# Channel attention with a squared-ReLU network: one sum and four softmax steps placed behind two PSUM additions, a bank copy ahead of a rounding step, a maximum ahead of four sums

## The chip, the core and the metric

One core of one Trainium2 chip runs the kernel. The metric is device time in microseconds (us), the median of three runs. TensorE (PE in the profile) multiplies, VectorE (DVE) and ScalarE (ACT) work on tiles, GpSimd (POOL) and SyncE (SP) issue the DMAs.

## What is computed

```
B, N, C = 4, 6080, 256;  d_ff = 2048;  everything float32
qn = q / (norm(q, axis=1) + 1e-6);  kn = k / (norm(k, axis=1) + 1e-6)
s  = kn^T @ qn / tau                       # 256 x 256 for each batch
a  = softmax over the last axis of s (max taken out, 1e-9 added to the sum)
x  = v @ a                                 # 6080 x 256 for each batch
out = max(x @ w_in, 0)^2 @ w_out           # w_in 256 x 2048, w_out 2048 x 256
```

## The kernel before

The attention matrix a and w_in of a batch are multiplied first (W = a w_in), so that the network runs on v itself: h = v W, out = max(h, 0)^2 w_out. A product in float32 is made of three products of rounded parts: each operand is split into a high part (a rounding cast, mostly on ACT) and a low part (the difference, on DVE).

v is cut into 48 blocks of 512 tokens (480 in the last two blocks of a batch), and the 2048 hidden channels into four groups of 512. The first two blocks and the last are done by plain products. The 45 blocks between make 180 **periods**, one for each block and group of channels. A period computes its piece of h with seven products in place of eight (a Strassen scheme), six matmuls of 128 x 256 for each, in three PSUM banks that the trace calls ps_b, ps_h and ps_c. The order in `period` (lines 1250 to 1334) is:

1. the first product into ps_b; ACT copies the bank to ps_c (the **bank copy**, "COPY ps_c<-ps_b") because later products add to both;
2. a product into ps_h, copied by ACT to the tile x; then a window of products with w_out for an earlier period (`window_S`, ps_o);
3. a product on top of ps_c, one on top of ps_b, one on top of ps_h; DVE adds ps_h to x (the **H addition**, "x<-x,ps_h");
4. a product on top of ps_c; DVE adds ps_c to x (the **C addition**, "x<-x,ps_c");
5. the products with w_out for the last period's rounded squares A (`window_A`), a last product on top of ps_c, which may begin only when the C addition has read the bank, and another window of products with w_out (`window_S` with the sums S).

Relu and square turn x into the squares. Beside their own rounding (`hi_A`, `lo_A`), sums of squares are needed for the windows S: `first_sums`, `third_sum` and `last_sum`, all on DVE ("x<-x" with nothing else), and the sums are split by `hi_S` (ACT, "s_hi") and `lo_S` (DVE, "s_lo<-x,s_hi"). `last_sum` finishes S1 and S2 of the period before (k-1). Where `plain(k - 1)` holds (the groups 0 and 1 of batches 0 to 2, and all groups in the first block) the sums are half as wide (256 elements for a partition instead of 512).

All engines keep the order in which the code records instructions. No scheduler moves them, so a line that is written earlier runs earlier on its engine, and an instruction that waits holds all that is behind it on that engine.

The softmax and W of the next batch (`softmax_and_W`) run beside the periods. The function is a generator: `yield from step(b, i, point)` hands control back until the period reaches a named point, and `side(point)` in `period` goes on with it there. The points come in the order "dve" (behind the first sums), "sq" (behind the C addition), "pe", "act" (before `window_A`), "mid" (behind the high part of A). Its steps: the maximum nx of the squared norms with a small number (reads the bank that the next period calls ps_b), three Newton steps for the inverse root of the norms, the inverse norms as a diagonal matrix (`diag`), the scaled scores, the negative row maximum (`negmax`), the exponentials, the reciprocal of their sum, and the transposed exponentials, cast to eT_hi and eT_lo (DVE) for the products with w_in (ps_w). In the trace the softmax of batch 1 stands at about 411 to 480 us, of batch 2 at 918 to 985 us, of batch 3 at 1422 to 1490 us.

The order written out in `period` that the change touches is this (from lines 1260 to 1315, shortened):

```
scalar.copy(C, B2)                     # bank copy
if prev and after_copy(k - 1): hi_A(k - 1, late_A)
...
third_sum(k - 1)
if plain(k - 1): last_sum(k - 1)
...
vector.tensor_add(s, s, H)             # H addition
if prev and not plain(k - 1): last_sum(k - 1)
product(k, C, S3, T3)
vector.tensor_add(s, s, C)             # C addition
side("sq")
lo_S(k - 1, "S1"); hi_S(k - 1, "S2")
square(k, a0)
```

In the trace nearly all instructions carry the line 27 of the recording layer; the tiles tell them apart. `hi_A` of a period is either called at its end or, where `after_copy` holds, in the next period behind the bank copy.

Of the kernel before, what the change touches and what calls it, by code (L numbers as in the profile page):

```python
# [8 lines left out]
F32 = mybir.dt.float32  # L9
# [21 lines left out]
def kernel(  # L31
# [22 lines left out]
    tensor, vector, scalar, pool_engine = (  # L54
        InProgramOrder(tc, e) for e in (nc.tensor, nc.vector, nc.scalar, nc.gpsimd)
    )
# [4 lines left out]
    NC = C // P  # L61
# [34 lines left out]
    small_tile = lambda name, b, cols, dt=F32: smalls.tile([P, cols], dt, tag=name, name=f"{name}{b}", bufs=1)  # L96
# [11 lines left out]
    def bank(name):  # L108

        at = banks["turn"] = (banks["turn"] + 1) % 3  # L110
        return ps_h.tile([P, T], F32, tag=f"h{at}", name=name)
# [72 lines left out]
    def switch_w_out(k):  # L184

        if k < GPB or k >= len(groups) or plain(k) == plain(k - GPB) or groups[k][2] in EARLY:
            return
        j = groups[k][2]
        if plain(k):
            reload_w_out(j)  # L190
            return
        for kept, part in zip(ws_kept[j], (wo_hi, wo_lo)):
            sync.dma_start(A21_of(part, j).bitcast(F32), kept)
# [123 lines left out]
    def reload_w_in(b, g):  # L317
        parts = wi_next[b, g] = wi_tiles(b, g)
        for kept, part in zip(wi_kept[g], parts):
            nc.sync.dma_start(part.bitcast(F32), kept)  # L320
# [208 lines left out]
    def until(point):  # L529

        while now["at"] != point:
            yield
# [53 lines left out]
    def step(b, first, point):  # L586

        if b == 0:
            for i in range(first):
                yield i > 0  # L590
        else:
            yield
            yield from until(point)

    def softmax_and_W(b):
# [4 lines left out]
        ps_n = ps_h.tile([P, T], F32, tag="h0", name=f"ps_n{b}") if b else bank(f"ps_n{b}")  # L600
        for m in range(2 * NC):
            tensor.matmul(
                ps_n[:, m : m + 1],
                acc[:, 1 - m // NC, 0, (m % NC) * P : (m % NC + 1) * P],
                ones[:, 0:1],
                start=m == 0,
                stop=True,
                skip_group_check=True,
            )
        yield from step(b, 2, "mid")  # L610
        if b:
            reload_w_in(b, 0)
        small = lambda name, dt=F32: small_tile(name, b, 2 * NC, dt)
        x = small("nx")

        vector.tensor_scalar_max(x, ps_n[:, 0 : 2 * NC], 2.0**-100)

        seed_i, y = small("nseed", I32), small("ny")
        vector.tensor_scalar(
# [7 lines left out]
            yield True  # L627
        for it in range(3):
            if it and b:
                yield from step(b, 1, "mid" if it == 1 else "dve")  # L630
            vector.tensor_mul(s_, x, y)
            vector.scalar_tensor_tensor(u_, s_, -0.5, y, op0=ALU.mult, op1=ALU.mult)
            vector.scalar_tensor_tensor(y, u_, 1.5, y, op0=ALU.add, op1=ALU.mult)
            if it == 1 and b == 0:
                yield False
# [16 lines left out]
        tensor.matmul(ps_b[:, 0:C], ones, diag.rearrange("p h c -> p (h c)"), start=True, stop=True)  # L652
        yield from step(b, 2, "mid")
        vector.tensor_mul(s, s, ps_b[:, 0:C].unsqueeze(1).broadcast_to([P, NC, C]))
        yield from step(b, 0, "dve")
        negmax = small_tile("negmax", b, NC)
        vector.tensor_reduce(negmax, s, axis=AX.X, op=ALU.max, negate=True)
        yield from step(b, 1, "act")
# [2 lines left out]
        for h in range(NC):  # L661
            scalar.activation(
                e[:, h, :], s[:, h, :], AF.Exp, bias=negmax[:, h : h + 1], accum_out=rsum[:, h : h + 1]
            )
        yield from step(b, 2, "dve")
        rinv = between.tile([P, NC], F32, tag="rinv", name=f"rinv{b}", bufs=1)
        vector.tensor_scalar_add(rsum, rsum, 1e-9)
        vector.reciprocal(rinv, rsum)
# [2 lines left out]
        for h in range(NC):  # L671
            for d in range(NC):
                tensor.transpose(
                    ps_t[:, d * C + h * P : d * C + (h + 1) * P], e[:, h, d * P : (d + 1) * P], ident
                )
        yield from step(b, 2, "dve")
        eT_hi = pool.tile([P, NC, C], F32R, tag="eT_hi", name=f"eT_hi{b}", bufs=1)
        eT_lo = pool.tile([P, NC, C], F32R, tag="s", name=f"eT_lo{b}", bufs=1)
        ps_tv = ps_t.rearrange("p (d c) -> p d c", d=NC)
# [278 lines left out]
    ORD = 1  # L958
    AT = (0, 0, 24, 26)
    AFTER_FROM = (12, 12, 12, 0)  # L960
    FREE_FROM = (12, 12, 12, 0)
    FREE = lambda k: groups[k][0] < B - 1 and groups[k][2] == 3 or groups[k][1] >= FREE_FROM[groups[k][0]]
    BS = (B - 1,)
# [5 lines left out]
    groups = [(b, n, j) for b, n in order[OLD:-1] for j in range(GPB)]  # L969
# [27 lines left out]
    def two_halves(tag, name):  # L997

        return ps_h.tile([P, 2, T // 2], F32, tag=tag, name=name)
# [5 lines left out]
    def half_of(k):  # L1005
        return blocks[groups[k][1]][1] // 2
# [34 lines left out]
    def plain(k):  # L1041

        b, n, j = groups[k]
        return (b, n) == order[OLD] if j in EARLY else n < FROM[j][b]
# [109 lines left out]
    a1, a0, a2, a3 = range(4)  # L1154

    def evict_C21(k):
        scalar.activation(XG[k][:, :, a2, :], C2.pop(k)[:, :, : half_of(k)], AF.Relu)
# [6 lines left out]
    def square(k, at):  # L1164
        s = XG[k][:, :, at, :]
        scalar.activation(s, s, AF.Square)

    def sum_of(k, to, one, other, op):

        x = XG[k][:, 0 : 1 if plain(k) else 2]  # L1170
        op(x[:, :, to, :], x[:, :, one, :], x[:, :, other, :])
# [8 lines left out]
    def third_sum(k):  # L1180
        sum_of(k, a2, a2, a1, vector.tensor_add)

    def last_sum(k):
        sum_of(k, a3, a3, a2, vector.tensor_sub)
# [10 lines left out]
    def hi_A(k, which):  # L1195
        s, at = which
        n = 1 if plain(k) else 2
        scalar.copy(PA[k, "A"][0][:, 0:n, at, :], XG[k][:, 0:n, s, :])
# [17 lines left out]
    def side(point):  # L1216

        now["at"] = point
        next(beside, None)
        if forming and next(forming[0], "end") == "end":  # L1220
            forming.pop(0)
# [23 lines left out]

    def after_copy(k):

        return not plain(k) and k < len(groups) - 1 and groups[k][1] >= AFTER_FROM[groups[k][0]]

    def period(k, before=nothing, w1=None, wa=None, w3=None):  # L1250

        now["k"] = k
        switch_w_out(k + 1)
        b, n, j = groups[k]
        half = half_of(k)
        prev = k > 0
        B2 = two_halves("h0", f"ps_b{k}")
        product(k, B2, A11, B11, start=True)
        C2[k] = C = two_halves("h2", f"ps_c{k}")
        scalar.copy(C[:, :, :half], B2[:, :, :half])  # L1260
        if prev and after_copy(k - 1):
            hi_A(k - 1, late_A)
        H = two_halves("h1", f"ps_h{k}")
        product(k, H, S1, T1, start=True)
        load_forms(k + 1, 1)
        x = XG[k] = pool.tile([P, 4, 2, half], F32, tag="x", name=f"x{k}").rearrange("p s r t -> p r s t")
        scalar.copy(x[:, :, a3, :], H[:, :, :half])
        if w1 is None and not plain(k - 2):
            copy_output(k - 2, 0)
        if prev:  # L1270
            if ORD and after_copy(k - 1):
                first_sums(k - 1)
                lo_A(k - 1, late_A)
            else:
                lo_A(k - 1, late_A)
                first_sums(k - 1)
        side("dve")
        late_step(last=True)
        if prev:
            third_sum(k - 1)  # L1280
            if plain(k - 1):
                last_sum(k - 1)
        v_step(k, "dve")
        (w1 or (lambda: window_S(k - 2, "S2")))()
        before()
        product(k, C, S2, T2)
        scalar.copy(x[:, :, a1, :], C[:, :, :half])
        if w1 is None:
            copy_output(k - 2, 0)
        load_forms(k + 2, 0)  # L1290
        late_step()
        if k >= len(groups) - 2:
            reload_w_out(k - len(groups) + 2)
        product(k, B2, A12, B21)
        if prev:
            hi_S(k - 1, "S1")
        scalar.activation(x[:, :, a0, :], B2[:, :, :half], AF.Relu)
        if w1 is None:
            copy_output(k - 2, 1)
        product(k, H, S4, B22)  # L1300
        s = x[:, :, a1, :]
        vector.tensor_add(s, s, H[:, :, :half])
        if FREE(k):
            scalar.activation(s, s, AF.Relu)
            square(k, a1)
        if prev and not plain(k - 1):
            last_sum(k - 1)
        product(k, C, S3, T3)
        s = x[:, :, a3, :]
        vector.tensor_add(s, s, C[:, :, :half])  # L1310
        side("sq")
        if prev:
            lo_S(k - 1, "S1")
            hi_S(k - 1, "S2")
        square(k, a0)
        relu_squares(k)
        if prev:
            lo_S(k - 1, "S2")
        side("pe")
        side("act")  # L1320
        v_step(k, "act")
        (wa or (lambda: window_A(k - 1)))()
        parts_tile(k, "A")
        hi_A(k, early_A)
        side("mid")
        v_step(k, "mid")
        lo_A(k, early_A)
        late_step()
        product(k, C, A22, T4)
        evict_C21(k)  # L1330
        square(k, a2)
        if not after_copy(k):
            hi_A(k, late_A)
        (w3 or (lambda: window_S(k - 1, "S1")))()
# [56 lines left out]
    for i in range(PAIR):  # L1391
        part = i % 2
        b, n, f = steps[i]
# [57 lines left out]
    for g in range(len(groups)):  # L1451
        b, n, j = groups[g]
# [16 lines left out]
    b, n = order[-1]  # L1469
# [77 lines left out]
```

## Time and profile before

| | |
|---|---|
| time, median of 3 runs | 2139.51 us (2138.34, 2139.51, 2139.69) |
| span of the profiled execution | 2137.0 us |
| time of the profiled execution itself | not listed apart; the median of the runs lies 2.5 us over its span |
| TensorE (PE) busy | 2123.9 us, 99%, 16990 matmuls |
| VectorE (DVE) busy | 1947.1 us, 91% |
| ScalarE (ACT) busy | 1818.6 us, 85% |
| GpSimd (POOL) busy | 403.4 us, 19% |
| chain that ended last | PE 89%, DVE 6%, ACT 2%, DMA 2%, issue 1% |

PE is busy in nearly the whole span. A row's duration overlaps the next row of its engine: matmuls of 256 columns are shown with .28 us and start every .12 us; DVE operations of 512 elements are shown with .68 us and start every .60 us. Times between rows are therefore taken from start to start.

### The profile page before, as it was taken

What the parts mean: (1) busy time and instruction counts of PE and PEld (TensorE: products, weight loads), DVE (VectorE), ACT (ScalarE), POOL (GpSimd) and SP (SyncE); (2) the same over time, 40 slices, a digit from 0 to 9 for tenths busy, and PEclk for the clock granted to TensorE, in tenths of its full rate; (3) what the DMA queues carried; (4) which work ended last, traced back from release to release, by engine and by line L of the source; (5) the groups of instructions that cost most, each with busy time, mean ns of one, the idle gap of its engine ahead of it and who ended that gap; (6) DMA issues with size and microseconds to landing.
All of it is one profiled execution on the core that took longest, in us unless ns stands there. A gap on an engine that the chain in (4) does not pass through costs nothing.

```text
span 2137.0 us, 43905 instructions
## 1 busy us (share of the span) xinstructions
PE 2123.9 (99%) x16990; PEld 2066.1 (97%) x16990; DVE 1947.1 (91%) x2577; ACT 1818.6 (85%) x2708; POOL 403.4 (19%) x506
## 2 busy tenths in 40 slices
PE   9999999999999999999999999999999999999999
PEld 8789999999999999999999999999999999999998
DVE  6898999998999999988999999999899999999993
ACT  5887888888888888878888888878888999999995
POOL 0000121211222121221222121121212122122121
PEclk9999999999999999999999999999999999999999
DMA  9777888889998888788999788887999788788783
GB/s 345 234 232 264 240 255 252 235 239 283 303 297 262 251 251 262 234 241 247 292 303 288 248 255 257 249 234 229 325 322 314 233 241 252 220 247 248 233 256 86
DMA packets 258865, 548.24 MB, mean 257 GB/s; under 512 B 26848, under 2 KB 120672, under 8 KB 258656
## 3 DMA queue, kind: packets, MB, share of 16 engines
q1 hardware_dynamic: 193696, 449.32, 62.3%
q0 software_dynamic: 64960, 96.11, 20.9%
q8 instruction: 134, 2.20, 0.4%
q14 instruction: 75, 0.61, 0.1%
HBM read 431.75 MB, written 64.23 MB: 232 GB/s over the span
## 4 chain that ended last, share of the span: by engine, by line
PE 89%; DVE 6%; ACT 2%; DMA 2%; issue 1%; SPq 0%; DVEq 0%; ACTq 0%
PE ps_o L27 41%; PE ps_c L27 16%; PE ps_h L27 14%; PE ps_b L27 11%; PE gram L27 4%; DVE x L27 2%; PE ps_w L27 2%; PE ps_o_m L27 1%; ACT x L27 1%; DMA wf<-wf_kept 1%; DVE s_lo L27 1%; DVE acc L27 1%; DMA qk<-in_k 1%; DVE A_lo L27 0%; DMA qk<-in_q 0%
## 5 line engine op out<-in xcount | busy, mean ns | idle before, releaser
L27 DVE TENSOR_TENSOR s_lo<-x,s_hi 128x1024 fp32r<-128x1024 f32 (+1 forms) x384 | 464.0, 1208 | 44.4 <-ACT s_hi L27 44.1
L27 PE MATMUL ps_c<-v_hi,wf 128*128 128x256 f32 (+1 forms) x2160 | 466.9, 280 | 4.4 <-DVE x L27 2.2
L27 POOL DMA_DIRECT2D o<-o x225 | 245.4, 1253 | 1102.7 <-ACT o L27 689.7
L27 ACT CAST s_hi<-x 128x1024 fp32r<-128x1024 f32 (+1 forms) x384 | 399.7, 1041 | 37.6 <-DVE x L27 27.9
L27 DVE TENSOR_TENSOR x<-x 128x1024 f32<-128x1024 f32 (+3 forms) x540 | 389.6, 722 | 10.3
L27 PEld LDWEIGHTS ps_c<-v_hi,wf 128*128 128x128 f32 x2160 | 367.4, 188 | 7.8 <-ACT ps_c L27 3.3
L27 ACT ACTIVATE x<-x 128x512 f32<-128x512 f32 (+2 forms) x540 | 350.0, 648 | 21.7 <-DVE x L27 9.2
L27 PE MATMUL ps_b<-v_hi,wf 128*128 128x256 f32 (+1 forms) x1440 | 309.7, 279 | 1.8 <-DVE nx L27 1.1
L27 PE MATMUL ps_h<-v_hi,wf 128*128 128x256 f32 (+1 forms) x1440 | 309.1, 278 | 0.0
L27 PE MATMUL ps_c<-v_lo,wf 128*128 128x256 f32 (+1 forms) x1080 | 300.9, 279 | 0.0
L27 DVE TENSOR_TENSOR A_lo<-x,A_hi 128x1024 fp32r<-128x1024 f32 (+3 forms) x360 | 276.9, 792 | 18.8 <-ACT A_hi L27 15.3
L27 ACT CAST A_hi<-x 128x1024 fp32r<-128x1024 f32 (+3 forms) x360 | 254.4, 707 | 38.4 <-DVE x L27 25.5
L27 PEld LDWEIGHTS ps_b<-v_hi,wf 128*128 128x128 f32 x1440 | 245.2, 188 | 2.3 <-DVE nx L27 1.3
L27 PEld LDWEIGHTS ps_h<-v_hi,wf 128*128 128x128 f32 x1440 | 244.9, 188 | 0.0
L27 ACT COPY x<-ps_c 128x512 f32<-128x512 f32 (+1 forms) x180 | 105.1, 584 | 158.3 <-PE ps_c L27 158.0
L27 PEld LDWEIGHTS ps_c<-v_lo,wf 128*128 128x128 f32 x1080 | 203.2, 188 | 0.1
L27 PE MATMUL ps_b<-v_lo,wf 128*128 128x256 f32 (+1 forms) x720 | 200.6, 279 | 0.0
L27 PE MATMUL ps_h<-v_lo,wf 128*128 128x256 f32 (+1 forms) x720 | 200.4, 278 | 0.0
L27 DVE TENSOR_TENSOR x<-x,ps_h 128x512 f32<-128x512 f32 (+1 forms) x180 | 122.4, 680 | 76.9 <-PE ps_h L27 76.6
L27 PE MATMUL ps_o<-s_hi,wo_hi 128*128 128x256 f32 (+3 forms) x954 | 190.1, 295 | 0.5 <-ACT s_hi L27 0.5
L27 PE MATMUL ps_o<-s_hi,wo_lo 128*128 128x256 f32 (+3 forms) x954 | 190.2, 295 | 0.0
L27 PE MATMUL ps_o<-s_lo,wo_hi 128*128 128x256 f32 (+3 forms) x954 | 190.0, 295 | 0.1
(166 smaller groups left out, 5166.9 us busy)
## 6 DMA issues: line engine op xcount, KB each, us to landing
wf<-wf_kept SPq DMA_DIRECT2D x360, 512.0 KB, 5.3
wf<-wf_kept SPq DMA_DIRECT2D x360, 384.0 KB, 4.9
o<-o POOLq DMA_DIRECT2D x114, 256.0 KB, 5.9
qk<-in_k SPq DMA_DIRECT2D x87, 256.0 KB, 4.3
qk<-in_q SPq DMA_DIRECT2D x87, 256.0 KB, 4.8
v<-in_vT POOLq DMA_DIRECT2D x76, 256.0 KB, 5.1
out_T<-o POOLq DMA_DIRECT2D x152, 128.0 KB, 4.7
o<-o POOLq DMA_DIRECT2D x76, 128.0 KB, 6.2
```

What stands on the lines that cost most here:

```text
L27: return lambda *args, **kwargs: self.tc.keep_in_program_order(issue(*args, **kwargs))
```

## The change

- `last_sum` of the period before is called behind both PSUM additions (H and C) for all periods, and the square of the part a0 (ACT) goes ahead of `hi_S(k - 1, "S2")`.
- Four of the softmax steps go from the point "dve" to the point "sq", which is now behind `last_sum`: the third Newton step with the diagonal, `negmax`, the reciprocal, and eT_hi with eT_lo.
- In the first nine periods `hi_A` of the period before stands behind the bank copy (`AFTER_FIRST`), and `first_sums` ahead of the late `lo_A`.
- nx is taken at the point "act" instead of "mid" for the batches 1 to 3.

```diff
+        small = lambda name, dt=F32: small_tile(name, b, 2 * NC, dt)
+        x = small("nx")
+        if b:
+            vector.tensor_scalar_max(x, ps_n[:, 0 : 2 * NC], 2.0**-100)
         yield from step(b, 2, "mid")
         if b:
             reload_w_in(b, 0)
-        small = lambda name, dt=F32: small_tile(name, b, 2 * NC, dt)
-        x = small("nx")
-
-        vector.tensor_scalar_max(x, ps_n[:, 0 : 2 * NC], 2.0**-100)
+        else:
+            vector.tensor_scalar_max(x, ps_n[:, 0 : 2 * NC], 2.0**-100)
...
-                yield from step(b, 1, "mid" if it == 1 else "dve")
+                yield from step(b, 1, "mid" if it == 1 else "sq")
...
-        yield from step(b, 0, "dve")
+        yield from step(b, 0, "sq")
         negmax = small_tile("negmax", b, NC)
...
-        yield from step(b, 2, "dve")
+        yield from step(b, 2, "sq")
         rinv = between.tile([P, NC], F32, tag="rinv", name=f"rinv{b}", bufs=1)
...
-        yield from step(b, 2, "dve")
+        yield from step(b, 2, "sq")
         eT_hi = pool.tile([P, NC, C], F32R, tag="eT_hi", name=f"eT_hi{b}", bufs=1)
...
+    AFTER_FIRST = 9
...
-        return not plain(k) and k < len(groups) - 1 and groups[k][1] >= AFTER_FROM[groups[k][0]]
+        return k < AFTER_FIRST or not plain(k) and k < len(groups) - 1 and groups[k][1] >= AFTER_FROM[groups[k][0]]
...
             third_sum(k - 1)
-            if plain(k - 1):
-                last_sum(k - 1)
         v_step(k, "dve")
...
-        if prev and not plain(k - 1):
-            last_sum(k - 1)
         product(k, C, S3, T3)
         s = x[:, :, a3, :]
         vector.tensor_add(s, s, C[:, :, :half])
+        square(k, a0)
+        if prev:
+            last_sum(k - 1)
         side("sq")
         if prev:
             lo_S(k - 1, "S1")
             hi_S(k - 1, "S2")
-        square(k, a0)
         relu_squares(k)
```

PE's order is the same in both programs, and so is POOL's. On VectorE at the step eT of batch 1 (period 28; x27 holds the squares and sums of period 27, x28 the tile of this period; ps_t1 the transposed exponentials) the order before is:

```order
L27 TENSOR_TENSOR x27_5402<-x27_5402 128x2x2x256
L27 CAST eT_hi1_5552<-ps_t1_5474 128x512
L27 TENSOR_TENSOR eT_lo1_5553<-ps_t1_5474,eT_hi1_5552 128x512
L27 TENSOR_TENSOR x27_5402<-x27_5402 128x512
L27 TENSOR_TENSOR x28_5548<-x28_5548,ps_h28_5537 128x512
L27 TENSOR_TENSOR x27_5402<-x27_5402 128x512
L27 TENSOR_TENSOR x28_5548<-x28_5548,ps_c28_5535 128x512
L27 TENSOR_TENSOR s1_lo_27_5587<-x27_5402,s1_hi_27_5586 128x1024
```

and with the change:

```order
L27 TENSOR_TENSOR x27_5402<-x27_5402 128x2x2x256
L27 TENSOR_TENSOR x27_5402<-x27_5402 128x512
L27 TENSOR_TENSOR x28_5548<-x28_5548,ps_h28_5537 128x512
L27 TENSOR_TENSOR x28_5548<-x28_5548,ps_c28_5535 128x512
L27 TENSOR_TENSOR x27_5402<-x27_5402 128x512
L27 CAST eT_hi1_5602<-ps_t1_5474 128x512
L27 TENSOR_TENSOR eT_lo1_5603<-ps_t1_5474,eT_hi1_5602 128x512
L27 TENSOR_TENSOR s1_lo_27_5583<-x27_5402,s1_hi_27_5582 128x1024
```

The two casts went from ahead of the third sum to behind the C addition and the last sum, while the products that read them (ps_w) keep their place on PE, directly behind the product that the C addition waits for. The same engine at the third Newton step of batch 1 (period 24), with the change (ns1 to nr1 and diag1 stood ahead of the second row, x23 128x512, before, and the fourth and third rows were in the other order):

```order
L27 TENSOR_TENSOR x23_4836<-x23_4836 128x512
L27 TENSOR_TENSOR x24_4971<-x24_4971,ps_h24_4960 128x512
L27 TENSOR_TENSOR x24_4971<-x24_4971,ps_c24_4958 128x512
L27 TENSOR_TENSOR x23_4836<-x23_4836 128x512
L27 TENSOR_TENSOR ns1_4777<-nx1_4754,ny1_4774 128x4
L27 SCALAR_TENSOR_TENSOR nu1_4778<-ns1_4777,ny1_4774 128x4
L27 SCALAR_TENSOR_TENSOR ny1_4774<-nu1_4778,ny1_4774 128x4
L27 TENSOR_TENSOR ns1_4777<-nx1_4754,ny1_4774 128x4
L27 TENSOR_SCALAR ns1_4777<-ns1_4777 128x4
L27 TENSOR_SCALAR ns1_4777<-ns1_4777,tau_sb_89 128x2
L27 RECIPROCAL nr1_5031<-ns1_4777 128x4
L27 TENSOR_SCALAR diag1_5033<-ident_82,nr1_5031 128x128 x2
```

Behind these rows stands s1_lo, the low part of S1. On ScalarE at the bank copy of period 8 (A_hi_7 is the rounding of period 7), before:

```order
L27 ACTIVATE x7_2437<-x7_2437 128x512
L27 CAST A_hi_7_2541<-x7_2437 128x2x256
L27 COPY ps_c8_2577<-ps_b8_2570 128x512
L27 COPY x8_2590<-ps_h8_2579 128x512
L27 COPY x8_2590<-ps_c8_2577 128x512
```

and with the change:

```order
L27 ACTIVATE x7_2437<-x7_2437 128x512
L27 COPY ps_c8_2576<-ps_b8_2569 128x512
L27 CAST A_hi_7_2541<-x7_2437 128x2x256
L27 COPY x8_2590<-ps_h8_2579 128x512
L27 COPY x8_2590<-ps_c8_2576 128x512
```

The copy and the rounding cast have changed places.

## Rows read from the trace of the kernel before

**Rows 1.** The profile page: its span, the busy time of each engine (with its share and number of instructions), and the granted TensorE clock in 40 slices, in tenths.

```profile
span 2137.0 us, 43905 instructions
PE 2123.9 (99%) x16990; PEld 2066.1 (97%) x16990; DVE 1947.1 (91%) x2577; ACT 1818.6 (85%) x2708; POOL 403.4 (19%) x506
PEclk9999999999999999999999999999999999999999
```

**Rows 2.** The waits of PE: what waited and for whom; us in total, times, longest.

```profile
PE ps_c L27 <- DVE x L27: 2.2, 5, 0.9
PE ps_c L27 <- ACT ps_c L27: 2.1, 3, 0.9
```

**Rows 3.** The timeline of VectorE in period 28, batch 1. Here and below the columns are start, duration, engine, line, operation, out<-in with its shape, count, and in brackets the idle time just before and what ended it.

```profile
476.01 0.69 DVE L27 CAST eT_hi<-ps_t 128x512 fp32r<-128x512 f32 x1
476.73 0.69 DVE L27 TENSOR_TENSOR eT_lo<-ps_t,eT_hi 128x512 fp32r<-128x512 f32 x1
...
477.94 0.68 DVE L27 TENSOR_TENSOR x<-x,ps_h 128x512 f32<-128x512 f32 x1
478.54 0.68 DVE L27 TENSOR_TENSOR x<-x 128x512 f32<-128x512 f32 x1
479.14 0.68 DVE L27 TENSOR_TENSOR x<-x,ps_c 128x512 f32<-128x512 f32 x1
```

**Rows 4.** The timeline of PE in the same period.

```profile
477.59 0.28 PE L27 MATMUL ps_c<-v_hi,wf 128*128 128x256 f32 x1
477.70 0.62 PE L27 MATMUL ps_w<-dec_w,eT_hi 128*128 128x512 f32 x2
478.16 0.61 PE L27 MATMUL ps_w<-dec_w,eT_lo 128*128 128x512 f32 x2
```

**Rows 5.** The timeline of PE and VectorE at the same step in batch 2.

```profile
983.68 0.28 PE L27 MATMUL ps_c<-v_hi,wf 128*128 128x256 f32 x1
...
984.00 0.69 DVE L27 TENSOR_TENSOR x<-x,ps_c 128x512 f32<-128x512 f32 x1
```

**Rows 6.** The timeline of VectorE around the third Newton step of batch 1, whose first row is ns at 432.70.

```profile
432.70 0.16 DVE L27 TENSOR_TENSOR ns<-nx,ny 128x4 f32<-128x4 f32 x1
...
434.56 0.69 DVE L27 TENSOR_TENSOR x<-x 128x512 f32<-128x512 f32 x1
...
436.96 1.22 DVE L27 TENSOR_TENSOR s_lo<-x,s_hi 128x1024 fp32r<-128x1024 f32 x1
438.10 1.22 DVE L27 SCALAR_TENSOR_TENSOR x<-x 128x1024 f32<-128x1024 f32 x1
```

**Rows 7.** The timeline of PE in the same period: the last product of the C addition, the last of window A, the product onto ps_c behind it, and the first that reads s_lo.

```profile
434.44 0.28 PE L27 MATMUL ps_c<-v_hi,wf 128*128 128x256 f32 x1
...
436.55 0.27 PE L27 MATMUL ps_o<-A_lo,wo_hi 128*128 128x256 f32 x1
437.10 0.39 PE L27 MATMUL ps_c<-v_hi,wf 128*128 128x256 f32 x1 [0.28 <-DVE x L27]
...
438.85 0.28 PE L27 MATMUL ps_o<-s_lo,wS_hi 128*128 128x256 f32 x1
```

**Rows 8.** The timeline of PE at the third Newton step of batch 2: the first product of window A and the first that reads s_lo.

```profile
942.81 0.39 PE L27 MATMUL ps_o<-A_hi,wo_hi 128*128 128x256 f32 x2
...
946.16 0.40 PE L27 MATMUL ps_o<-s_lo,wS_hi 128*128 128x256 f32 x2
```

**Rows 9.** The timeline of ScalarE at the bank copy of the period that follows the Newton step of batch 1.

```profile
441.23 0.41 ACT L27 CAST A_hi<-x 128x256 fp32r<-128x256 f32 x1
441.54 0.58 ACT L27 COPY ps_c<-ps_b 128x512 f32<-128x512 f32 x1
```

**Rows 10.** The timeline of PE there: the product onto ps_c that needs the copy.

```profile
442.17 0.39 PE L27 MATMUL ps_c<-v_hi,wf 128*128 128x256 f32 x1
```

**Rows 11.** The timeline of all engines where nx of batch 2 is taken.

```profile
924.92 1.80 DVE L27 TENSOR_TENSOR v<-v 128x256 f32<-128x256 f32 x4
...
925.46 0.28 PE L27 MATMUL ps_o<-s_lo,wo_hi 128*128 128x256 f32 x1
...
926.64 0.15 DVE L27 TENSOR_SCALAR nx<-ps_n 128x4 f32<-128x4 f32 x1
...
926.85 0.38 PE L27 MATMUL ps_b<-v_hi,wf 128*128 128x256 f32 x1 [1.11 <-DVE nx L27]
```

**Rows 12.** The timeline of all engines at a bank copy in the first nine periods.

```profile
250.85 0.62 ACT L27 CAST A_hi<-x 128x512 fp32r<-128x512 f32 x1
251.37 0.58 ACT L27 COPY ps_c<-ps_b 128x512 f32<-128x512 f32 x1
...
252.00 0.39 PE L27 MATMUL ps_c<-v_hi,wf 128*128 128x256 f32 x1 [0.92 <-ACT ps_c L27]
```

**Rows 13.** The timeline of VectorE and PE at a C addition whose last sum stood ahead of both additions.

```profile
615.00 0.89 DVE L27 TENSOR_TENSOR x<-x 128x256 f32<-128x256 f32 x2
...
616.40 0.68 DVE L27 TENSOR_TENSOR x<-x,ps_c 128x512 f32<-128x512 f32 x1
...
617.14 0.39 PE L27 MATMUL ps_c<-v_hi,wf 128*128 128x256 f32 x1 [0.42 <-DVE x L27]
```

**Rows 14.** The timeline of PE at a C addition in batch 3.

```profile
1689.00 0.28 PE L27 MATMUL ps_o<-A_lo,wo_hi 128*128 128x256 f32 x1
...
1689.19 0.39 PE L27 MATMUL ps_c<-v_hi,wf 128*128 128x256 f32 x1
```

## The prediction

> **What bounds the kernel now.** I read the page first. PE is busy in 2123.9 of 2137.0 us, 99% [rows 1], so time can be won or lost only where PE stands still. PE's order does not change; what the change can do is to move the moments at which VectorE and ScalarE release PE. The next view is therefore the waits of PE: the largest behind the start are products onto ps_c, 2.2 us in five waits for DVE's C addition and 2.1 us in three waits for ACT's bank copy [rows 2]. That is all that the moved sums and copies can win, apart from nx below and waits too short for that view. Then the timelines of the places that the edits touch, start to start, for PE and the engine that releases it. The rates I use from them: a matmul of 256 columns starts every .12 us and one of 512 columns every .23 [rows 4]; a VectorE step of 512 elements takes .60 (477.94 to 478.54) [rows 3], two sums of 256 together .80 [rows 13], a pass of 1024 takes 1.14 [rows 6]. The C addition starts .32 behind the start of the last product (983.68 to 984.00) [rows 5]. PE starts about .05 behind the end of what it waited for, and after a wait the next product comes about .11 later than the pace (437.10 carries .39 instead of .28) [rows 7].
>
> **The change part by part.** A positive number is time lost.
>
> *eT behind the last sum: +7.0.* Before, eT_hi starts at 476.01, over a microsecond ahead of the products that read it, at 477.70 [rows 3, 4]. Now it stands behind the C addition and the last sum, while ps_w stays directly behind the product that the C addition waits for. The last product starts at 477.59 [rows 4], the C addition at 477.91, the last sum at 478.51, eT_hi at 479.11; with its .69 [rows 3] and .05 PE goes on at 479.85 instead of 477.70: 2.15 of standing still. eT_lo comes .72 behind eT_hi [rows 3], while PE has only two products of .23 to do before it needs it: another .25 with the restart. Together 2.4. In batch 2 the last sum is half as wide: 984.00 + .60 + .40 + .69 + .05 = 985.74, against 983.80 [rows 5], 1.95 and .25, 2.2. Batch 3 has the same shape as batch 1, 2.4. Nothing covers this, since nothing that is ready stands on PE between the product and ps_w. Bounds 5.6 (no restart costs, C addition at once) to 7.6.
>
> By the rows a VectorE step of 512 elements holds its engine for .60 although its row says .68 to .69 [rows 3]; I use the starts. The Trainium skill, "VectorE: DVE Perf Modes", section "The DRAIN you can't avoid", says that the next operation does not start until the pipe is empty; by it, with the rows' full durations, the two steps ahead of eT_hi would each take .08 more, and this term would be about 7.5. The trace disagrees, since successive starts here are closer than one duration.
>
> *Third Newton step and diagonal behind the last sum: +1.7.* The block is 1.86 long (432.70 to 434.56) [rows 6]. It left room ahead of the H addition, which now begins earlier; but it goes ahead of s_lo. In batch 1: last product 434.44 [rows 7], C addition 434.76, last sum 435.36, block 435.96, s_lo 437.82 to 439.04, so PE can read it at 439.09. It needs it at 438.85 [rows 7], but .55 of that was a wait at 436.55 to 437.10 [rows 7], which is gone since the C addition is no longer behind the last sum: .43 and the restart. So need 438.30, wait .79 and restart .11, less .55: +.35. Batch 3 alike. In batch 2 the last product is at 942.69, one step ahead of window A [rows 8]; C addition 943.01, last sum 943.61, block 944.01, s_lo 945.87 to 947.09, PE at 947.14 against 946.16 [rows 8]: +1.0 with restart less a small wait saved. Sum 1.7, bounds .5 to 2.5.
>
> *What follows the late steps: +2.0.* The squares of the period (438.10) [rows 6] start at 438.95, .85 later; on ACT the rounding of A and the bank copy of the next period (441.54) [rows 9] follow. The product that needs the copy stood at 442.17 [rows 10] with a short wait; moved by .35 it would be at about 442.35, and the copy comes at 442.98 or so: about +.5. The same in batch 3, +.3 in batch 2 where PE has already waited more: together about 1.2. negmax is one pass over 512 elements, .60 by the row nearest to it [rows 3], in front of s_lo in the three batches; between nothing and all of it I take .27 each, .8. The reciprocal is of four numbers at most and is nothing beside it. Bounds 0 (ACT's slack takes it all) to 3.0.
>
> *nx ahead of v: -1.4.* In batch 2 nx, which frees the bank of ps_b, stood behind four sums of v (924.92 to 926.64), and PE stood from 925.46 to 926.85, 1.39 less a pace of .12 plus a restart of .1 [rows 11]. Now nx is issued ahead of them, about 1.7 earlier, and PE goes on without a wait. Batches 1 and 3 have no such row, 0. Bounds -1.4 and -1.0. The four sums move .2 back and are waited for by nothing near.
>
> *The C addition without the last sum ahead: -1.9.* At 616.40 the C addition stands behind two sums [rows 13]; one, .40, goes behind it, and PE at 617.14 waited .42 by its bracket: I take -.4 there and -.3 at a like place at 1629. In batch 3 nine places have a PE step from the last of window A to the next product onto ps_c of .19 or so instead of .12, and the next one a restart later [rows 14]: -.07 to -.18, together -1.2. Bounds -2.5 to -.7. In periods without such a wait the last sum goes from one place to another of the same engine, in front of s_lo. VectorE's idle time ahead of the H addition becomes longer and the time behind shorter by .60; s_lo is read some 1.9 us behind the product before window A (436.96 to 438.85) [rows 6, 7], so s_lo at the same time as before costs nothing.
>
> *Bank copy ahead of the rounding in nine periods: -1.1.* PE's three waits for this copy are 2.1 us [rows 2]; the brackets count from the modelled end, .16 behind the pace, and each has a restart, so 2.9 is the most there is. The copy goes ahead of one cast: .52 at 250.85 [rows 12], .31 where it is narrow [rows 9]. I take -.52 and twice -.31. The cast itself is then later by the copy's .52, and with it A_lo on VectorE, which is why I don't take more. Bounds -3.0 and 0.
>
> *Sum.* 7.0 + 1.7 + 2.0 - 1.4 - 1.9 - 1.1 = +6.3. Against the span of 2137.0, with the same 2.5 us outside it, that is 2143.3 and **2145.8** us as a time; the median of the runs, 2139.5, is that span with its 2.5.
>
> **The rivals.** A measurement of this kernel can tell some 0.2% from no change: 4.3 us, that is below 2135.2 or above 2143.8.
>
> *The copies and squares are in time.* The early squares on ACT and earlier copies make the follow-on 0, and the first nine periods give all of 2.9: 6.3 - 2.0 - 1.8 = +2.5, **2142.0**, not slower. For it: ACT is busy for 85% of the span [rows 1], and the first wait at each copy is a chain of ScalarE steps that gets shorter. Against: near 441 ACT's row order shows no room between cast and copy [rows 9].
>
> *eT is hidden.* If PE does not need eT directly behind the product, for example because ps_c's last product comes much later than in the rows, the 7.0 go: -.7, **2138.8**. Against: the order shows the same neighbours, and rows 4 and 5 have no gap.
>
> *The waits fall and eT is hidden.* The other side: the C addition decides more waits than the view names, since it stands in front of a product in all 180 periods; from the point at which eT_hi is ready by the time that PE has finished the product, the sum is 0 for the late steps and -1.4 - 1.9 - 2.9 = -6.2 or more, up to -8 with the last sum's .60 gained elsewhere: about **2132**, faster. For it: 2.2 us in five waits are named [rows 2]. Against: it needs VectorE over two microseconds ahead.
>
> *The clock falls.* The granted clock reads 9 in all slices, the upper level (2.4 GHz) [rows 1], though PE stood 1.39 us at a stretch [rows 11]. The new pauses are 2.15. If each brings PE to 1.2 GHz for about the length of a window A and the rest of its period, some 4 us, three times 4 us is +12: **2158**. The Trainium skill, "TensorE: Matmul & The Clock Gate", "Part 1: The HAM clock gate", says that the clock falls to its lower level after PE has idled; by it a pause could cost more than its length. No row of this trace shows it falling behind a pause.
>
> *The change does not do what it says.* Excluded by the order of the instructions, which shows each of the moves.
>
> **How the numbers follow.** The forecast, 2143.8 to 2148.5 by the bounds of its terms taken together: .52, and .04 for more of the same kind. Copies in time (2142.0, between 2139.5 and 2143.8): .22. eT hidden (2138.8): .09. The waits fall (2132): .10. The clock: .03. Slower is .52 + .04 + .03 = .59, same .22 + .09 = .31, faster .10. The range leaves out the fast case, the clock and the end of the forecast: 2138.0 to 2149.5.
>
> **What would show it.** Right: three waits "ps_w for DVE eT" of 1.9 to 2.2 us in the waits of PE, and VectorE's eT_hi behind the last sum; no wait for nx at 926; waits of s_lo of .8 to 1.1 behind the third Newton step; fewer waits of ps_c for DVE x. Wrong: no wait at ps_w, or a C addition that starts late in the other periods; PE's waits for ACT's copy as large as before would put the time at the upper end.

## The result

The changed kernel takes **2154.2 us** (median of 5 runs, 2151.7 to 2157.5); the kernel before took 2139.7 in its five. The ratio is 1.0070, with a 95% interval of 1.0057 to 1.0082: 14.5 us slower. The forecast was 2145.8, with a range to 2149.5: the direction was right, the size was not, and the time lies beyond the range.

The profiled execution has a span of 2153.7 us, 16.7 more than before; its own time is 2155.5, 1.3 above the median. These are its page's lines that answer to [rows 1], and after them the waits of PE (what waited, for whom; us in total, times, longest), which answer to [rows 2].

```profile
span 2153.7 us, 43914 instructions
PE 2131.0 (99%) x16990; PEld 2072.1 (96%) x16990; DVE 1942.8 (90%) x2577; ACT 1827.2 (85%) x2708; POOL 402.9 (19%) x506
PEclk9999999999999999999999999999999999999999
```

```profile
PE ps_w L27 <- DVE eT_lo L27: 7.9, 3, 2.7
PE ps_o L27 <- DVE s_lo L27: 2.2, 3, 0.9
PE gram L27 <- DMA qk<-in_q: 1.7, 2, 1.3
PE ps_c L27 <- ACT ps_c L27: 1.7, 4, 0.6
PE gram L27 <- DVE qk_lo L27: 1.4, 3, 0.9
...
PE ps_c L27 <- ACT x L27: 0.7, 1, 0.7
...
PE ps_c L27 <- DVE x L27: 0.4, 1, 0.4
```

Three new things are at the top: the three stops ahead of ps_w, the three of s_lo, and gram behind qk_lo. The waits for the C addition (DVE x) fell from 2.2 to .4, and the wait for nx is gone, but the waits for the bank copy (ACT ps_c) hardly fell. PE busy rose by 7.1 us with the same number of matmuls: some of them ran slower.

VectorE and PE at the step eT of batch 1, which answer to [rows 3, 4]:

```profile
478.42 0.69 DVE L27 TENSOR_TENSOR x<-x,ps_h 128x512 f32<-128x512 f32 x1 [0.43 <-PE ps_h L27]
479.05 0.69 DVE L27 TENSOR_TENSOR x<-x,ps_c 128x512 f32<-128x512 f32 x1
479.65 0.69 DVE L27 TENSOR_TENSOR x<-x 128x512 f32<-128x512 f32 x1
480.26 0.69 DVE L27 CAST eT_hi<-ps_t 128x512 fp32r<-128x512 f32 x1
480.98 0.69 DVE L27 TENSOR_TENSOR eT_lo<-ps_t,eT_hi 128x512 fp32r<-128x512 f32 x1
```

```profile
478.74 0.27 PE L27 MATMUL ps_c<-v_hi,wf 128*128 128x256 f32 x1
481.72 0.73 PE L27 MATMUL ps_w<-dec_w,eT_hi 128*128 128x512 f32 x2 [2.71 <-DVE eT_lo L27]
482.29 0.63 PE L27 MATMUL ps_w<-dec_w,eT_lo 128*128 128x512 f32 x2
482.75 0.94 PE L27 MATMUL ps_w<-acc_w,eT_hi 128*128 128x512 f32 x2
483.50 1.06 PE L27 MATMUL ps_o<-A_hi,wo_hi 128*128 128x256 f32 x4
484.35 0.41 PE L27 MATMUL ps_o<-A_hi,wS_hi 128*128 128x256 f32 x1
```

VectorE's order and its distances from PE's last product are as the prediction has them, to .01 us. But PE does not go on when eT_hi ends at 480.95; it goes on when eT_lo ends. From 478.74 to 481.72 are 2.98, 2.87 over the pace. And then four products of 256 columns take .85 instead of .47: they start every .21 us. The windows over these places (start and end, length, busy time and number of PE, PEld, DVE, ACT and POOL, then the granted clock, DMA share, GB/s) show why:

```profile
479.00:481.60 2.60, 0.01 (x1) 0.00 (x0) 2.56 (x6) 1.71 (x3) 0.00 (x0) 1.00 0.61 233
481.60:486.30 4.70, 4.58 (x20) 4.21 (x21) 4.61 (x7) 0.69 (x2) 0.00 (x0) 0.64 0.03 11
...
994.00:998.30 4.30, 4.30 (x21) 4.03 (x20) 4.30 (x5) 2.35 (x3) 0.21 (x1) 0.60 0.34 54
...
1504.50:1509.00 4.50, 4.50 (x32) 4.23 (x33) 4.43 (x6) 1.33 (x3) 0.00 (x0) 1.00 0.00 0
```

Behind the stops of batches 1 and 2 the mean granted clock is .64 and .60, so most of these 4.5 us ran at 1.2 GHz; behind that of batch 3, as long as that of batch 1, it is 1.00. The page's clock row, with slices of 54 us, shows 9 throughout; such a fall is seen only in a window of its own size.

From start to start, taking the same matmuls in both traces, the terms of the sum measure as follows:

| term | forecast | measured |
|---|---|---|
| stops at eT, three batches | +7.0 | +8.8 (3.1, 2.7, 3.0) |
| matmuls at half the clock behind them | 0 | +3.0 (1.5, 1.5, 0) |
| third Newton step ahead of s_lo | +1.7 | +1.8 (.35, 1.05, .4) |
| late copies in the softmax stretches | +2.0 | +2.6 |
| nx in batch 2 | -1.4 | -1.5 |
| C addition at the places that the prediction names (two, and nine in batch 3) | -1.9 | -2.0 (.4, .4, 1.2) |
| new waits for the bank copy outside the softmax stretches (525, 652, 1101, 1546 us) | 0 | +1.3 |
| first nine periods | -1.1 | -.1 |
| slower pace of the matmuls in batch 3 | 0 | +2.3 |
| waits for DMAs that vary between executions (start, 579, 1136 us) | 0 | -.1 |

That is 16.1 of 16.7; the rest is in gaps of under .2 us. The row on the pace is the sum of all differences of under .06 us from one matmul to the next in batch 3.

### The profile page after: what moved, and what is told of

Read it like the earlier page. It is cut to its first block, busy times and chain, and to the rows that moved or that the text cites. A ratio compares the mean times of both kernels' runs of the same rounds, so it can differ in the third digit from the quotient of the medians.

```text
span 2153.7 us, 43914 instructions
## 1 busy us (share of the span) xinstructions
PE 2131.0 (99%) x16990; PEld 2072.1 (96%) x16990; DVE 1942.8 (90%) x2577; ACT 1827.2 (85%) x2708; POOL 402.9 (19%) x506
## 4 chain that ended last, share of the span: by engine, by line
PE 89%; DVE 6%; ACT 2%; DMA 1%; issue 1%; SPq 0%; DVEq 0%; ACTq 0%
PE ps_o L27 40%; PE ps_c L27 16%; PE ps_h L27 13%; PE ps_b L27 11%; PE gram L27 6%; DVE x L27 2%; PE ps_w L27 2%; PE ps_o_m L27 1%; DVE s_lo L27 1%; DMA wf<-wf_kept 1%; ACT x L27 1%; DVE A_lo L27 0%; ACT A_hi L27 0%; ACT s_hi L27 0%; DVE wo_sums L27 0%
## 5 line engine op out<-in xcount | busy, mean ns | idle before, releaser
L27 ACT ACTIVATE x<-x 128x512 f32<-128x512 f32 (+2 forms) x540 | 341.6, 646 | 25.8 <-DVE x L27 11.1
```

The costliest lines, as they stand in the source:

```text
L27: return lambda *args, **kwargs: self.tc.keep_in_program_order(issue(*args, **kwargs))
```

## The experiments

All ran on the chip beside new runs of the kernel before, whose medians were 2138.6 to 2138.9. Each expectation weighs two theories of its own.

**eT back.** The changed kernel with one word changed:

```
-        yield from step(b, 2, "sq")
+        yield from step(b, 2, "dve")
         eT_hi = pool.tile([P, NC, C], F32R, tag="eT_hi", name=f"eT_hi{b}", bufs=1)
```

> The changed kernel with only the step eT_hi/eT_lo back at its old point, ahead of the third sum. Theory 1 (the place of eT costs most: in the profile after, PE stands 2.6 to 2.9 us at the first product of ps_w in three batches, and in two of them the next 20 matmuls run at half the granted clock, 11.7 us together): span 2142, time about 2144, no wait at ps_w, granted clock 1.00 in all of 475 to 500 us. Theory 2 (VectorE is full there, and what it does not lose at eT it loses at the next bank copy or low part): 2149 or more, with new waits of 1 us or more for A_hi or s_lo right behind.

Measured: 2141.8 us, 1.0015 of the kernel before (1.0005 to 1.0025). No wait at ps_w is left, the granted clock is 1.00 from 475 to 500 us, and no new wait of 1 us stands behind the step. The one word takes back 12 of the 14.5 us. Theory 2, that VectorE loses the time behind the step instead, falls.

**eT alone.** The same word the other way in the kernel before.

> The kernel before with only the eT step moved behind the C addition, the last sum left where it was. Theory 1: eT_lo ends at the same moment as in the changed kernel, since the last sum then stands ahead of the C addition instead of behind it; three stops of 2.6 to 2.9 us, 8.5 together, and 0 to 1.5 us each from the clock: 2148 to 2152. Theory 2: the stop needs the moved last sum too, so it is shorter by its .60 and the clock stays up: 2145 to 2147.

Measured: 2151.5 us, 1.0062 (1.0047 to 1.0077), 12.9 us above the kernel before. The waits of PE in this execution begin with

```profile
PE ps_w L27 <- DVE eT_lo L27: 7.5, 3, 2.7
```

so the stop does not need the moved last sum. From start to start the stops are 2.84, 2.27 and 2.84; the clock fell behind the first and the third here, not behind the second.

**eT split.** In the changed kernel eT_hi goes back to "dve" and eT_lo stays behind the last sum:

```
         vector.tensor_copy(eT_hi, ps_tv)
+        yield from step(b, 0, "sq")
         vector.tensor_sub(eT_lo, ps_tv, eT_hi.bitcast(F32))
```

with `step(b, 2, "dve")` ahead of eT_hi.

> The changed kernel with eT_hi back at its old point and eT_lo alone left behind the last sum. Theory 1 (the first product of ps_w does not wait for eT_hi, but for the bank: ps_t, which eT_lo reads, and ps_w share one): PE still stops ahead of the first product of ps_w, .6 to .7 us shorter than the 2.87 of the changed kernel, so 2.1 to 2.3 in batches 1 and 3, and the time is 2 us below the changed kernel if the granted clock still falls, up to 5 if it no longer does: 2147 to 2152. Theory 2 (the products wait for their operands, as the prediction had it): no stop ahead of the first product, 1.7 us ahead of the third, which reads eT_lo: 2145 to 2147.

Measured: 2148.2 us, 1.0046 (1.0032 to 1.0059). VectorE and PE in batch 1:

```profile
477.31 0.69 DVE L27 CAST eT_hi<-ps_t 128x512 fp32r<-128x512 f32 x1
...
480.38 0.68 DVE L27 TENSOR_TENSOR eT_lo<-ps_t,eT_hi 128x512 fp32r<-128x512 f32 x1
```

```profile
478.86 0.28 PE L27 MATMUL ps_c<-v_hi,wf 128*128 128x256 f32 x1
481.12 0.72 PE L27 MATMUL ps_w<-dec_w,eT_hi 128*128 128x512 f32 x2 [1.98 <-DVE eT_lo L27]
```

eT_hi has ended at 478.00, .86 before PE's last product ahead of ps_w starts; yet the first product of ps_w, which reads eT_hi alone, waits for eT_lo. What it waits for is not its operand. ps_t and ps_w are allocated one after the other under the tag "gram" (the helper `later` in `softmax_and_W`), and the tag has one bank: the product may overwrite ps_t only when eT_lo has read it. That the product waits for eT_lo is shown; that the shared bank is the reason is read from the code, since no run gives ps_w a bank of its own. The stop is 2.14, 1.87 and 2.15 us, shorter by the .72 of eT_hi: theory 1. In this profile the clock fell behind the first of the three.

**Filled stops.** Twelve products that nobody reads stand in the stop, in a bank that is free:

```
             yield from until("pe")
+            if g == 0:
+                busy = ps_h.tile([P, T], F32, tag="h0", name=f"busy{b}")
+                for i in range(12):
+                    tensor.matmul(busy[:, 0:GRP], hi[:, 0, 0:P], hi[:, 0, :], start=True, stop=True)
             products(0)
```

> The changed kernel with 12 matmuls of 512 columns, whose result nobody reads, issued on PE ahead of the first product of ps_w in each of batches 1 to 3 (2.8 us, about the length of the stop). Theory 1 (the granted clock falls because PE stands still for nearly 3 us): clock 1.00 behind ps_w in all three batches, no row of .41 for 256 columns there, the time 1.5 to 4 us below the changed kernel in the same call, about 2151, and nearly no spread between runs. Theory 2 (the clock falls for another reason): windows of about .6 remain, and the time is that of the changed kernel or up to 1 us more.

Measured: 2149.4 us, 1.0057 (1.0040 to 1.0074), below the 1.0070 of the change though PE has 8.4 us more of work. The windows behind the filled stops:

```profile
477.80:483.00 5.20, 5.12 (x26) 4.17 (x26) 5.17 (x8) 2.39 (x4) 0.00 (x0) 1.00 0.42 157
987.00:993.00 6.00, 5.92 (x33) 4.97 (x32) 5.54 (x8) 3.19 (x5) 1.19 (x1) 1.00 0.63 172
1497.00:1503.00 6.00, 5.93 (x34) 4.98 (x32) 5.97 (x8) 2.92 (x5) 0.00 (x0) 1.00 0.34 122
```

The clock stays at 1.00 in all three. Three of the four times lie within 1.2 us, close to what theory 1 expected; the fourth, 2153.7, is that of the profiled execution, with a stop of 2.0 us that hangs on a DMA (below). The intervals of the two ratios overlap, so the time alone would not show the gain; the windows do.

**The third Newton step back.** `"mid" if it == 1 else "dve"` in the changed kernel.

> The changed kernel with only the third Newton step and the diagonal back at their old point. Theory 1 (the block holds s_lo, and with it the next period's squares): the three waits of ps_o for s_lo, 2.2 us in the profile of the changed kernel, go, and the waits at the bank copy behind them become shorter by at most .5 each: 2.2 to 4 us below the changed kernel, 2150 to 2152. Theory 2 (the copies behind are late through the moved last sum, not through this block): the waits for s_lo go, the .56 us at the bank copy behind them stay, 2152.

Measured: 2150.9 us, 1.0060 (1.0046 to 1.0074), 2 to 3 us below the change, with intervals that overlap. In its trace the waits for s_lo are gone, but PE still waits .56 for the copy at 440.8 us: on that point theory 2 is right, and this late copy does not come from the block. The one behind the step in batch 2 (957 us in the change) does: its .35 is gone.

**All four steps back.** The word "dve" in all four places; last sum, nx and the first nine periods as changed.

> The changed kernel with all four softmax steps back at their old points; last_sum behind both additions, nx and the copy of the first nine periods stay. Theory 1: eT 11.7, third Newton step 1.8 and the late steps behind it 2.6 are gone, 2153.7 - 16.1 = 2137.6 of span, 2139 to 2140 as a time, the same as before. Theory 2 (the moved last sum is what costs, through later low parts in all periods): 2145 or more.

Measured: 2137.1 us, .9993 (.9984 to 1.0003). The four moved steps are the whole loss.

**The last sum alone**, in the kernel before:

```
             third_sum(k - 1)
-            if plain(k - 1):
-                last_sum(k - 1)
...
-        if prev and not plain(k - 1):
-            last_sum(k - 1)
         product(k, C, S3, T3)
...
+        square(k, a0)
+        if prev:
+            last_sum(k - 1)
         side("sq")
...
-        square(k, a0)
         relu_squares(k)
```

> The kernel before with only the last sum (and the square of a0) behind both additions; the four steps, nx and the first nine periods as before, so that three of the steps at their old point stand where they were. Theory 1 (gains at the C addition are paid back at the bank copy, because the squares of the period come .6 later on VectorE where it has no idle time): waits for DVE x fall from 2.2 to under .6 us, waits for ACT's copy do not fall but stand at 441, 474, 519, 645 and 1453 us, .3 to .8 each: within 1 us of the kernel before. Theory 2 (as predicted, periods without a wait lose nothing): 1.9 us or more below it.

Measured: 2138.6 us, .9999 (.9990 to 1.0008). Its waits of PE, and the copy behind the third Newton step, which answers to [rows 10]:

```profile
PE ps_c L27 <- ACT ps_c L27: 3.1, 6, 0.9
PE ps_c L27 <- DVE x L27: 1.9, 2, 1.4
```

```profile
441.24 0.39 PE L27 MATMUL ps_c<-v_hi,wf 128*128 128x256 f32 x1 [0.40 <-ACT ps_c L27]
```

The .55 at 436.55 [rows 7] is gone, and .67 stands at 441 in its place; .30 at 474 became .80. New waits of .25 to .29 stand at 518, 644 and 1529, one of .47 at 1454. (The 1.4 for DVE x is one stop at 1904 us that hangs on a DMA, below.) Theory 1: in these stretches PE waits at the copy for what it no longer waits for at the C addition. Its reason, that the squares come .6 later on VectorE, does not hold at 441: counted from PE's product ahead of the C addition, s_lo, the squares and the copy come where they came before, to .03 us, and behind the copy PE is where it was before, to .01. At 518, 644 and 1529, where PE did not wait before, the copy is later by .3 to .5. In batch 3 nothing is paid back: the nine waits like [rows 14] are gone, 1.2 us together.

**The first nine periods alone**: `AFTER_FIRST = 9` and its use in `after_copy`, in the kernel before.

> The kernel before with only the bank copy of the first nine periods ahead of the rounding cast. Theory 1 (the stretch is full on VectorE, and what PE wins at the copy it loses at the low part of qk, which comes behind the later casts): waits of PE for ACT's copy fall from 2.1 to about .5 us, waits of gram for qk_lo rise by 1 us or more; within .5 of the kernel before. Theory 2 (as predicted): 1.1 us below it.

Measured: 2138.7 us, 1.0005 (.9996 to 1.0014).

```profile
PE gram L27 <- DVE qk_lo L27: 1.8, 3, 1.1
...
PE ps_c L27 <- ACT ps_c L27: 0.6, 3, 0.3
```

The copy's 2.1 [rows 2] became .6, and the products of gram wait 1.8 us for qk_lo. Theory 1.

**nx alone**, in the kernel before:

> The kernel before with nx alone taken at the earlier point. Theory 1: the wait of ps_b for nx in batch 2, 1.1 us by the bracket and 1.4 from start to start, is gone and nothing takes its place: 1.4 us below the kernel before. Theory 2 (the four sums of v, now behind nx, hold the low part of A): the wait moves to A_lo in the next period, no change beyond .3.

Measured: 2136.4 us, .9992 (.9983 to 1.0001), 2.2 below. The wait for nx is gone in the profile, and nothing stands at the next A_lo. The interval just takes in no change; the profile decides for theory 1.

**nx and the last sum in batch 3 only.** As above, with the last sum behind both additions where `b == B - 1` and in its old place elsewhere.

> The kernel before with nx earlier and with the last sum (and the square of a0) behind both additions in the last batch alone, where no softmax runs beside and VectorE has room. Theory 1: 1.4 us for nx and 1.2 us for the short waits at nine C additions of batch 3, nothing given back: 2.6 us below the kernel before, about .9988. Theory 2 (the small loss of pace in batch 3 has nothing to do with the C addition, or the bank copies there become late instead): 1.4 us below it.

Measured: 2136.0 us, .9987 (.9978 to .9995): the one version that is faster than the kernel before beyond its interval. Whether batch 3 adds to nx cannot be told from the times, .9992 and .9987. In its trace the nine waits are gone, 1.2 us together, and yet PE lost .4 us more in batch 3 than before: its matmuls ran at the slower of two paces in 12 of 18 stretches, before in 7 (next section).

## Why the prediction was wrong

**The step that failed is the first term, eT, and with it the clock.** It said that PE goes on when eT_hi is ready, 2.15 us late, and waits .25 more for eT_lo. The stop is 2.87: PE waits for both casts at once, because ps_w overwrites the bank from which eT_lo reads. The order of instructions on VectorE and their times were right; what was missed is the second thing that releases a matmul, the readers of the bank it overwrites. eT_split shows the wait for eT_lo. That mis-sizes the term by 1.8 us. A little of it is arithmetic: by the prediction's own rows the second wait is .72 less .46, .26, and the restart behind it .11, so .37 and not .25.

**The rival on the clock had .03 and came true in two of three places.** It was argued down by "No row of this trace shows it falling behind a pause." But the longest pause of that trace is 1.39 us [rows 11]; it had nothing to say of 2.9. In the twelve profiles here, counted beyond 185 us, PE stood still for 1.5 us or more 18 times (1.57 to 2.87); ten of these were followed by matmuls at half the clock, which lost 1.4 to 1.6 us each time. None of the stops of 1.31 or less was. Length alone doesn't decide: 2.87 fell in batch 1 and not in batch 3 of the same execution. The price guessed in that rival, 4 us a stop, was over twice too high. The Trainium skill, "TensorE: Matmul & The Clock Gate", "Part 1: The HAM clock gate", says that the clock is at its lower level after PE has idled. The runs agree where they show a fall, with mean clocks of .64 and .60 behind the stops of batches 1 and 2; behind eight of the 18 stops there was none.

**The C addition gave what was forecast; what came beside it was missed.** At 623 and 1645 us .4 each are gone, forecast as .4 and .3, and at the nine places of batch 3 the 1.2 that was forecast: in all eight traces with the moved sum there, and in none of the other three. The step that failed is "costs nothing", said of s_lo in the periods without such a wait. Ten periods got a wait of .1 to .3 for the copy; four of them, outside the softmax stretches, make the +1.3. In the first nine periods the copies gave 2.2, more than forecast, and gram's products, which wait for qk_lo, took back 1.7; .3 more went at a copy behind them (297 us). In the kernel before VectorE is busy in 70.71 of the 74 us from 187 to 261 us (first nine periods) and in 53.63 of the 55 from 430 to 485 us: what PE won at one place it lost at the next that VectorE releases, directly or through ACT. The share alone does not tell where that happens, since in batch 3, where nothing came back, it is 359.29 of 380 us, nearly as high.

**The pace in batch 3 does not follow the change.** No term of the forecast stood for this +2.3, and it hides the 1.2. Windows of 250 us in batch 3, of the kernel before, the change and four_back, with the number of matmuls behind PE's busy time:

```profile
1650.00:1900.00 250.00, 250.00 (x2134) 249.50 (x2133) 235.28 (x292) 232.63 (x355) 53.54 (x70) 1.00 0.80 242
```

```profile
1666.00:1916.00 250.00, 250.00 (x2129) 250.00 (x2129) 235.27 (x292) 231.73 (x353) 53.46 (x70) 1.00 0.80 241
```

```profile
1650.00:1900.00 250.00, 250.00 (x2147) 250.00 (x2147) 237.32 (x294) 233.96 (x357) 54.34 (x71) 1.00 0.82 244
```

The change and four_back run the same instructions there, and the granted clock is 1.00 in all. Matmul by matmul there are two paces, .1167 us and .1178 from start to start for 256 columns, each kept for tens of us. Of 18 stretches of 20 us (1670 to 2030 us of the kernel before) the kernel before has 7 at the slower pace, the change all 18, four_back, eT_back and newton_back none. What sets the pace stays open.

**What was right.** nx (-1.4 forecast, -1.5 measured):

```profile
932.33 0.28 PE L27 MATMUL ps_o<-s_lo,wo_hi 128*128 128x256 f32 x1
932.44 0.28 PE L27 MATMUL ps_b<-v_hi,wf 128*128 128x256 f32 x1
```

.11 from one product to the next, where 1.39 stood [rows 11]. The third Newton step (1.7 against 1.8) came out as worked out, s_lo behind the block and PE's wait of .9 with its restart:

```profile
437.55 1.22 DVE L27 TENSOR_TENSOR s_lo<-x,s_hi 128x1024 fp32r<-128x1024 f32 x1
```

```profile
437.90 0.28 PE L27 MATMUL ps_o<-s_hi,wo_lo 128*128 128x256 f32 x1
438.82 0.38 PE L27 MATMUL ps_o<-s_lo,wS_hi 128*128 128x256 f32 x1 [0.64 <-DVE s_lo L27]
```

(PE is .28 earlier here than in the kernel before, so 437.55 is 437.83 on its scale, forecast as 437.82.)

**What was right in part by luck.** The late copies in the softmax stretches (+2.0 against 2.6) had about the right size. In batch 2 the copy behind the Newton step is .35 late because of the step, as forecast (.3). In batches 1 and 3 it is .5 late, as forecast, but for another reason: it stays in newton_back and stands in sum_alone, so it comes from the moved last sum. The .8 put down to negmax as waits for s_lo came as late copies behind it, .3 in each batch (465, 977 and 1488 us); they are gone in four_back and stay in newton_back, so they come from the moved steps behind Newton. Which of them is not shown, since no run moves negmax alone.

In all, 16.7 is 10.4 more than 6.3: 1.8 for the bank, 3.0 for the clock, 1.3 for the new waits at copies, .6 for the late copies, 1.0 for the first nine periods and 2.3 for the pace; what else differs is within 1 us. The forecast's band of 2143.8 to 2148.5 is narrower than its bounds: taken together these give -.8 to +11.4 us, and 14.5 lies beyond them too. Its late copies, .5, .5 and .3, are 1.3 together and not 1.2.

## What to carry to other kernels

Before a step is put behind others, list everything that its successors on PE wait for: operands, and the readers of the bank or tile that they overwrite. A wait that can be taken away is a gain only if the next product that the same engine releases, directly or through another, does not then wait instead: work that one out too, above all where the engine has hardly any idle time. And a stop on PE that is longer than any in the trace before can have a second price, the clock behind it, for which that trace gives no bound.

## What else the runs showed

The times of one version spread by 1.8 to 7 us. Only one execution of each has a trace, so the cause is not shown for the others; but the traces hold stops that hang on DMAs, of another length in each, and in some none. Most of the longest stand at 571 to 580 us (a store to out_T, where the trace names one) and at 1899 to 1914 us (a load of v). In eT_back VectorE stood 2.7 us for a load of v, and PE for 1.6 us at 1907 us with a fall of the clock behind it; in fill ACT's copy of an output stood 2.5 us until the tile's earlier store to out_T was done, and PE for 2.0 us:

```profile
1902.60 1.80 DVE L27 TENSOR_TENSOR v<-v 128x256 f32<-128x256 f32 x4 [2.72 <-DMA v<-in_vT]
```

```profile
1678.63 0.96 ACT L27 COPY o<-ps_o 128x960 f32<-128x960 f32 x1 [2.47 <-DMA out_T<-o]
```

So one profile's span can hold 2 to 4 us that have nothing to do with the change, and the pace in batch 3 another 2, about as much as the terms that were disputed here; they were told apart by naming each stop, not by the span.
